# A gated mix of linear attention and a state-space convolution: one group's accumulating transfers, cast and triangle product at other places of the order

## The chip, the cores and the metric

One NeuronCore of one Trainium2 chip runs the kernel. The metric is device time in microseconds (us) of one launch. Three runs of the kernel before gave 176.87, 177.70 and 178.03 us, median 177.7 us.

The core has five engines that each work through their own instructions in order: PE (TensorE, matrix products), ACT (ScalarE), DVE (VectorE), POOL (GpSimd) and SP (SyncE, which here only issues transfers). POOL can issue transfers too. A waiting instruction holds back everything behind it on its engine.

## What is computed

```python
g = sigmoid((x * gate_w).sum(-1, keepdims=True))      # x: 1 x 2048 x 448
# a: linear attention, 16 heads of 28
phi = lambda t: where(t > 0, t + 1, exp(t)) + 1e-6
pq, pk = phi(q), phi(k)                               # q, k, v from x @ wqkv
o = (pq @ sum_s(pk * v)) / (pq @ sum_s(pk) + 1e-6)    # not causal
a = o @ wo
# b: convolution of every channel over all 2048 rows, by FFT in the reference
K = 2 * Re(sum_n C * exp(A * dt * l));  b = conv(x, K) + x * D_skip
out = g * a + (1 - g) * b
```

For the parameters of a channel the kernel tests whether all taps of K are the same number to float32. Where they are, the convolution of that channel is this tap times the running sum of x over the rows. This is what the main path computes; a second function, `general_conv`, runs only if the test fails for some channel.

## The kernel before, in words

The 2048 rows are cut into 16 chunks of 128. Four chunks make a group; chunk 4g+r holds, on partition p, row 512g+4p+r. So the four chunks of a group lie side by side as rows r = 0 to 3 of one partition. float32 products are made from a rounded high part (cast on ACT) and the remainder (subtraction on POOL or DVE), so each projection of a chunk is 11 matrix products of 128x448.

**The main loop** (line 517, c = 2 to 13) does, for each c, on PE: the projection k of chunk c+1 (`project`, L349; its result lies in the PSUM bank "k", for c = 2 and 4 in "v1"), the projection q of chunk c, and the products `do_g(c)` (L425), which add x(c) times the feature phi(k(c)) to four sums. PE is given these three blocks of 11 products one after the other, in every round. Around them stand:

- `load_x(c+3)` (L210): SP loads a later chunk, 512 KB, into one of four buffers.
- `split_t(c+2)` (L250, then L246) and `split_n` (L256, then L246): ACT casts the transposed and the plain chunk, POOL subtracts. `skip(c)` (L262) on POOL puts x times D_skip into y.
- `k_feature`, `k_high`, `k_low` (L376 to L388): two activations on ACT, one DVE pass in place in the bank "k", then the cast `pkh` on ACT and two more DVE passes that read the bank. Until the last of them the bank can't take the next projection k.
- `q_post` (L396 to L403): the same for q, with three or four activations on ACT.
- `steps`: pieces of the test of the taps (`s4d_prepare`). Its last reads of the parameters are the DVE instructions L305, two in c = 2 and two in c = 3.

**The running sum** goes group by group, with five steps whose places in the loop are the subject here:

1. `group_load(g)` (L432, SP): 896 KB of x into a home of the group: `wvo` for group 0, `pq` for 1, `room` for 2, `spare` for 3. Home 1 is the place of the parameters that L305 reads, so its load waits for L305, and SP with it.
2. `running_a(g)` (L436) and `running_b(g)` (L440): accumulating transfers of 448 KB issued by POOL. The first adds rows 0 and 2 to rows 1 and 3, the second adds row 1 to rows 2 and 3. The second waits for the first to land, on POOL.
3. `group_split(g)` (L444 on ACT, L246 on POOL): the high and low part of row 3, the tile `sums`.
4. `group_heads(g)` (L451, PE): a triangle matrix times `sums`, two products; they give what all earlier partitions add.
5. `convolve(c)` (L456, L457, DVE), twice for a group: adds the heads, multiplies by the tap; then `group_add(g)` (L463) adds the group to y by a transfer.

After the loop the kernel closes the sums, forms the attention matrices, and goes through the 16 chunks once more with transposes (L647), products `a` (L673) and the writing of the output.

The order of all instructions is written by hand (`manual_schedule`): each engine gets them in the order of the Python text. Before, group 0 stands in it thus: `running_a(0)` last in c = 2 (after `split_n(4)`), `running_b(0)` in c = 4 after `split_t(6)`, `group_split(0)` in c = 5 between the two activations of k(6) and `pkh(6)`, `group_heads(0)` last in c = 5, `convolve(0)` at the head of c = 6.

Of the kernel before, what the change touches and what calls it, by code (L numbers as in the profile page):

```python
# [32 lines left out]
QW = 512  # L33
EDGE = 16
G = 4
PAIRS = (2, 4, 5, 6)
HALVES = (4, 6, 7, 9)
SMALL = 2.0 ** -70
FLAT = 2.0 ** 35
BIG = 3.4028234e38  # L40
# [107 lines left out]
def gated_mix_kernel(ctx: ExitStack, tc: tile.TileContext, xin, wq_d, wvo_d, abc_d, ldt_d, dsk_d,  # L148
# [58 lines left out]
    def load_x(c):  # L207
        r = xp.tile([P, XC], F32, name="xr", tag="xr")
        turned[c], plain[c] = r[:, :NAT], r[:, NAT:]
        SP.dma_start(out=r, in_=xin[c])  # L210
# [34 lines left out]
    def low(eng, o, r, h):  # L245
        eng.tensor_tensor(out=o, in0=r, in1=h.bitcast(F32), op=ALU.subtract)  # L246

    def split_t(c):
        w = xt[c] = xt_p.tile([P, 2 * NAT], F32R, name="xt", tag="t")
        ACT.copy(w[:, :NAT], turned[c])  # L250
        low(POOL, w[:, NAT:], turned[c], w[:, :NAT])

    def split_n(c, both=True):
        r, w = plain[c], xn_p.tile([P, NX], F32R, name="xn", tag="n")
        xn[c] = w
        ACT.copy(w[:, :XC - NAT], r)  # L256
        if c > 2 and both:
            skip(c)
        low(POOL, w[:, XC - NAT:], r[:, :D], w[:, :D])

    def skip(c):
        POOL.tensor_tensor(out=y[:, c], in0=plain[c][:, :D], in1=dsk, op=ALU.mult)  # L262
# [68 lines left out]
    def pieces(c, wh, wl, n, tag, last=None):  # L331
        o = ps.tile([P, 512], F32, name=tag, tag=tag)
        h, l = ([xt[c][:, i + k * P:i + (k + 1) * P] for k in range(J)] for i in (0, NAT))
        hh, lh, hl = ([(a[k], w[:, k]) for k in range(J)] for a, w in ((h, wh), (l, wh), (h, wl)))
        hl = hl[1:]
        if last == "x":
            seq = hh + hl + lh
        else:
            seq = [p for k in range(J) for p in (hh[k], lh[k])] + hl
            if last and len(last) > 1:  # L340
                seq = [{"h": hh, "l": lh, "w": [None] + hl}[i[0]][int(i[1])] for i in last.split()]
            elif last == "w":
                seq = seq[2:6] + seq[8:9] + seq[6:8] + seq[9:] + seq[:2]

        def run(count):
            for _ in range(min(count, len(seq))):
                a, b = seq.pop(0)
                run.n += 1
                PE.matmul(o[:, :n], lhsT=a, rhs=b, start=run.n == 1, stop=not seq)  # L349
        run.n = 0  # L350
        return o, run

    def project(*args, **kw):
        o, run = pieces(*args, **kw)
        run(11)
        return o
# [16 lines left out]
    def k_feature(c, o):  # L373
        e = tp.tile([P, D], F32, name="e", tag="e")
        pks[c] = o[:, :D]
        ACT.activation(e, pks[c], AF.Relu, scale=-1.0)  # L376
        ACT.activation(e, e, AF.Exp, scale=-1.0)  # L377
        DVE.scalar_tensor_tensor(out=pks[c], in0=pks[c], scalar=1.0, in1=e, op0=ALU.add, op1=ALU.max)  # L378

    def k_high(c):  # L380
        pkh[c] = tp.tile([P, 512], F32R, name="pkh", tag="pkh")[:, EDGE:EDGE + D]
        ACT.add(pkh[c], pks[c], 1e-6)

    def k_low(c):
        pk = pks.pop(c)
        pkl[c] = tp.tile([P, 512], F32R, name="pkl", tag="pkl")[:, EDGE:EDGE + D]
        for o, a, op in ((pkl[c], pkh[c].bitcast(F32), ALU.subtract), (zb, zb, ALU.add))[::-1 if c > 6 else 1]:
            DVE.scalar_tensor_tensor(out=o, in0=pk, scalar=1e-6, in1=a, op0=ALU.add, op1=op)  # L388
# [6 lines left out]
    def q_post(c, o, mid=None):  # L395
        ACT.activation(e1[:, c:c + 1], o[:, D:D + 1], AF.Exp, scale=-1.0)  # L396
        if c < 5 or c >= NC - 2:
            return feature(pq[:, c], o, mid, side[0][:, :D] if 1 < c < 5 else None)
        e = tp.tile([P, D], F32, name="e", tag="e")
        ACT.activation(e, o[:, :D], AF.Relu, scale=-1.0)  # L400
        ACT.activation(e, e, AF.Exp, scale=-1.0)
        ACT.add(e, e, 1e-6)
        DVE.scalar_tensor_tensor(out=pq[:, c], in0=o[:, :D], scalar=C1, in1=e, op0=ALU.add, op1=ALU.max)  # L403
# [27 lines left out]
    def group_load(g):  # L431
        SP.dma_start(out=homes[g], in_=xin[g * G:(g + 1) * G, :, NAT:LO].rearrange("r p d -> p r d"))  # L432

    def running_a(g):
        w = homes[g]
        POOL.dma_start(out=w[:, 1::2], in_=w[:, 0::2], accum_op=ALU.add)  # L436

    def running_b(g):
        w = homes[g]
        POOL.dma_start(out=w[:, 2:], in_=w[:, 1:2].to_broadcast([P, 2, D]), accum_op=ALU.add)  # L440

    def group_split(g):
        w = sums[g] = tp.tile([P, 2, D], F32R, name="sums", tag="v0", bufs=1)
        ACT.copy(w[:, 0], homes[g][:, G - 1])  # L444
        low(POOL, w[:, 1], homes[g][:, G - 1], w[:, 0])

    def group_heads(g):
        o = heads[g] = ps.tile([P, 512], F32, name="v", tag="v0")[:, :D]
        w = sums.pop(g)
        for i in range(2):  # L450
            PE.matmul(o, lhsT=tri, rhs=w[:, i], start=i == 0, stop=i == 1)  # L451

    def convolve(c):
        g, i = c // G, c % G
        a, full = homes[g][:, i:i + 2], [P, 2, D]
        DVE.tensor_tensor(out=a, in0=a, in1=heads[g][:, None, :].to_broadcast(full), op=ALU.add)  # L456
        DVE.tensor_tensor(out=a, in0=a, in1=near[0][:, None, :].to_broadcast(full), op=ALU.mult)  # L457
        if i and g < NC // G - 1:
            for k in (g, UL + g):
                SP.dma_start(out=u[k:k + 1], in_=homes[g][P - 1:P, G - 1])  # L460

    def group_add(g):
        POOL.dma_start(out=y[:, g * G:(g + 1) * G], in_=homes[g], accum_op=ALU.add)  # L463

    prep = s4d_prepare()
    def steps(n):
        for _ in range(n):
            next(prep, None)
# [48 lines left out]
    for c in range(2, NC - 2):  # L517
        if c + 3 < NC:
            load_x(c + 3)
        if c == 2:  # L520
            SP.dma_start(out=cst, in_=cst_d)
        if c == 10:
            SP.dma_start(out=wo, in_=wvo_d[:DJ, 1])
        if c == 11:
            SP.dma_start(out=wv, in_=wvo_d[:, 0])
        ko = project(c + 1, wkh, wkl, D, "v1" if c in (2, 4) else "k")
        if c > 5:
            convolve(2 * c - 12)
        split_t(c + 2)
        if c in HALVES:  # L530
            running_b(HALVES.index(c))
        if c > 5:
            split_n(c + 2, False)
        k_feature(c + 1, ko)
        if c in (5, 7, 9, 11):
            group_split(c // 2 - 2)
        if c > 5:
            skip(c + 2)
        k_high(c + 1)
        k_low(c + 1)  # L540
        qo = project(c, wqh, wql, D + 2, "q")
        q_post(c, qo)
        if c < 5:
            steps(2 if c == 4 else 1)
        if c == 4:
            ACT.copy(tri, trir)
            ACT.copy(gcr, gcat)
        if c == 7:
            SP.dma_start(out=okr[:, None, :DJ], in_=oks[:, None, :])
        if c == 9:  # L550
            DVE.tensor_reduce(out=okr[:, DJ:], in_=okr[:, :DJ], op=ALU.add, axis=AX.X)
            DVE.tensor_copy(okn, okr[:, DJ:])
        do_g(c, (0, 1))
        if c == 5:
            steps(1)
        do_g(c, (2, 3))
        if c in (5, 7, 9, 11):
            group_heads(c // 2 - 2)
        if c < 4:
            skip(c - 1)  # L560
        if c < 6:
            split_n(c + 2)
        if c in (3, 4, 5):
            group_load(c - 2)
        if c in PAIRS:
            running_a(PAIRS.index(c))
        if c in (7, 9, 11, 13):
            group_add(c // 2 - 3)
        for j in {12: (0, 1), 13: (2, 3)}.get(c, ()):
            w = xn_p.tile([P, NX], F32R, name="wo", tag="n") if j < 2 else xp.tile([P, XC], F32R, name="wo", tag="xr")  # L570
            w = w[:DJ, :2 * D].rearrange("p (i d) -> p i d", i=2)
            woh.append(w[:, 0])
            wol.append(w[:, 1])
            ACT.copy(woh[j], wo[:, j])
            low(POOL, wol[j], wo[:, j], woh[j])
# [110 lines left out]
    c = NC - 2  # L686
# [291 lines left out]
```

## Time and profile before

| | |
|---|---|
| median of three runs | 177.7 us (176.87 to 178.03) |
| the profiled execution, its own time | 178.07 us |
| its span, first to last instruction | 176.2 us |
| PE busy | 165.9 us, 94% of the span, 852 matrix products |
| PE weight loads, beside the products | 148.5 us, 84% |
| POOL busy | 119.4 us, 68% |
| DVE busy | 117.2 us, 67% |
| ACT busy | 107.6 us, 61% |
| moved by DMA | 29.45 MB, 7.34 MB of it in transfers issued by POOL |

The profile counts from the span's start. "L246" is a line of the kernel; "xt<-xr" are tiles, written and read. A bracket behind a row gives the idle time of the engine before it and what ended it. The 1.87 us between the execution's own time and its span lie outside the instructions.

### The profile page before, as it was taken

The numbers are of one execution on the slowest core, as the hardware profiler recorded it, in microseconds if no ns is written. First come the engines' busy times: TensorE is split into PE (matmuls) and PEld (weight loads), VectorE is DVE, ScalarE is ACT, GpSimd is POOL, SyncE is SP. The second block draws the span as 40 slices with busy tenths as digits, with TensorE's granted clock in tenths as the row PEclk, the third lists the DMA queues.
The fourth block names the chain that finished last, engine by engine and source line by source line (L and its number), as shares of the span: only waits on it lengthen the run. The fifth ranks groups of instructions, "written<-read, shape, count | busy, mean of one in ns | idle before, by whom it ended". The sixth has DMA issues, their size and how long they took to land.

```text
span 176.2 us, 2710 instructions
## 1 busy us (share of the span) xinstructions
PE 165.9 (94%) x852; PEld 148.5 (84%) x852; DVE 117.2 (67%) x230; ACT 107.6 (61%) x245; POOL 119.4 (68%) x128
## 2 busy tenths in 40 slices
PE   6999999999927999999999999999999999999990
PEld 2698999989915999999999999999879999999990
DVE  0837736598416476585775676877888998997541
ACT  3778488894217669469478586665664564675441
POOL 6082688799517999949837929839886997954000
PEclk9999999999996999999999999999999999999999
DMA  5999997056999999958999820630031221221221
GB/s 178 404 301 272 255 287 293 14 92 179 271 264 346 337 184 195 290 119 173 288 274 302 180 56 0 130 80 0 5 67 54 105 105 57 103 102 57 106 107 57
DMA packets 12186, 29.45 MB, mean 167 GB/s; under 512 B 1549, under 2 KB 8410, under 8 KB 12170
## 3 DMA queue, kind: packets, MB, share of 16 engines
q1 hardware_dynamic: 9274, 21.81, 38.2%
q0 software_dynamic: 2752, 7.34, 21.9%
q8 instruction: 7, 0.11, 0.3%
q10 hardware_dynamic: 144, 0.11, 0.2%
q14 instruction: 9, 0.07, 0.1%
HBM read 17.93 MB, written 3.67 MB: 123 GB/s over the span
## 4 chain that ended last, share of the span: by engine, by line
PE 59%; ACT 8%; DMA 8%; DVE 4%; POOL 3%; issue 2%; SPq 1%; ACTq 0%; POOLq 0%; DVEq 0%
PE a L673 19%; PE q L349 11%; PE g L425 11%; PE k L349 11%; DMA wvo<-wvo 7%; PE tr L647 3%; DMA wk<-shl 2%; ACT y L303 2%; PE v L349 1%; ACT y L304 1%; PE v L451 1%; POOL xt L246 1%; ACT xn L256 1%; SPq L810 1%; POOL xn L246 1%
## 5 line engine op out<-in xcount | busy, mean ns | idle before, releaser
L673 PE MATMUL a<-wk,th 128*128 128x448 f32 (+1 forms) x170 | 36.7, 361 | 0.2 <-DMA wk<-shl 0.2
L425 PE MATMUL g<-pkh,xn 128*128 128x448 f32 x112 | 35.8, 364 | 0.0
L673 PEld LDWEIGHTS a<-wk,th 128*128 128x128 f32 x170 | 29.5, 189 | 2.3 <-issue 0.7
L246 POOL TENSOR_TENSOR xt<-xr,xt 128x512 fp32r<-128x512 f32 x14 | 21.3, 1521 | 12.6 <-ACT xt L250 12.6
L349 PE MATMUL k<-wk,xt 128*128 128x448 f32 x121 | 28.5, 383 | 0.0
L349 PE MATMUL q<-wqh,xt 128*128 128x450 f32 x120 | 27.6, 367 | 0.0
L246 POOL TENSOR_TENSOR xn<-xr,xn 128x448 fp32r<-128x448 f32 x16 | 22.8, 1424 | 4.8 <-ACT xn L256 4.8
L349 PEld LDWEIGHTS k<-wk,xt 128*128 128x128 f32 x121 | 23.9, 198 | 2.4 <-ACT wk L473 0.5
L349 PEld LDWEIGHTS q<-wqh,xt 128*128 128x128 f32 x120 | 22.5, 189 | 1.8
L425 PE MATMUL g<-pkl,xn 128*128 128x448 f32 x64 | 23.4, 366 | 0.0
L425 PEld LDWEIGHTS g<-pkh,xn 128*128 128x128 f32 x112 | 21.1, 188 | 2.2
L262 POOL TENSOR_TENSOR y<-xr,rows 128x448 f32<-128x448 f32 x16 | 22.1, 1414 | 0.0
L585 POOL TENSOR_TENSOR room<-pq,zb 128x448 f32<-128x448 f32 x16 | 18.7, 1173 | 3.8 <-ACT zb L707 2.7
L610 POOL TENSOR_TENSOR room<-pq,den 128x336 f32<-128x336 f32 x16 | 12.3, 769 | 7.5 <-ACT den L599 4.0
L378 DVE SCALAR_TENSOR_TENSOR k<-k,e 128x448 f32<-128x448 f32 x11 | 7.0, 632 | 15.0 <-ACT e L377 15.0
L678 DVE SCALAR_TENSOR_TENSOR ot<-y,og,a 128x448 f32<-128x448 f32 (+1 forms) x17 | 10.7, 629 | 5.5 <-PE a L673 5.5
L376 ACT ACTIVATE e<-k 128x448 f32<-128x448 f32 x11 | 6.0, 544 | 12.3 <-PE k L349 12.3
L655 DVE TENSOR_TENSOR th<-tr,th 128x512 fp32r<-128x512 f32 x16 | 11.0, 690 | 2.6 <-ACT th L654 2.0
L654 ACT CAST th<-tr 128x512 fp32r<-128x512 f32 x16 | 9.4, 588 | 5.1 <-PE tr L647 4.9
L425 PEld LDWEIGHTS g<-pkl,xn 128*128 128x128 f32 x64 | 11.2, 174 | 1.2 <-DVE pkl L388 0.2
L349 PE MATMUL v<-wk,xt 128*128 128x448 f32 x55 | 12.0, 364 | 0.0
L250 ACT CAST xt<-xr 128x512 fp32r<-128x512 f32 x14 | 8.6, 611 | 5.7 <-DMA xr<-in 5.7
(183 smaller groups left out, 321.1 us busy)
## 6 DMA issues: line engine op xcount, KB each, us to landing
xr<-in SPq DMA_DIRECT2D x15, 512.0 KB, 4.4
out<-ot SPq DMA_DIRECT2D x15, 224.0 KB, 1.9
pq<-in SPq DMA_DIRECT2D x4, 448.0 KB, 13.7
wvo<-in SPq DMA_DIRECT2D x2, 896.0 KB, 12.4
y<-in SPq DMA_DIRECT2D x2, 480.0 KB, 4.0
y<-in SPq DMA_DIRECT2D x2, 450.0 KB, 7.8
wvo<-wvo POOLq DMA_DIRECT2D x2, 448.0 KB, 8.2
pq<-in SPq DMA_DIRECT2D x1, 896.0 KB
```

The source lines that it names most:

```text
L246: eng.tensor_tensor(out=o, in0=r, in1=h.bitcast(F32), op=ALU.subtract)
L250: ACT.copy(w[:, :NAT], turned[c])
L262: POOL.tensor_tensor(out=y[:, c], in0=plain[c][:, :D], in1=dsk, op=ALU.mult)
L349: PE.matmul(o[:, :n], lhsT=a, rhs=b, start=run.n == 1, stop=not seq)
L378: DVE.scalar_tensor_tensor(out=pks[c], in0=pks[c], scalar=1.0, in1=e, op0=ALU.add, op1=ALU.max)
L425: PE.matmul(g[i][:a.shape[1], :D], lhsT=a, rhs=b, start=c == 0 and n == 0, stop=c == NC - 1 and n == len(seq) - 1)
L585: POOL.tensor_tensor(out=pd[c], in0=pq[:, c], in1=zb, op=ALU.mult)
L610: POOL.tensor_tensor(out=n[:, :3, :DJ].rearrange("p j (h d) -> p j h d", h=4), in0=a, in1=r[:, :H - 4].rearrange("p (j h) -> p j h", j=3)[ ...
L654: ACT.copy(h, ov)
L655: DVE.tensor_tensor(out=l, in0=ov, in1=h.bitcast(F32), op=ALU.subtract)
L673: PE.matmul(a[:, lo:hi], lhsT=u_, rhs=w_[:, lo:hi], start=n == 0, stop=n == 10)
L678: DVE.scalar_tensor_tensor(out=ot[:, lo:hi], in0=y[:, c, lo:hi], scalar=og[:, c:c + 1], in1=a[:, lo:hi], op0=ALU.mult, op1=ALU.add)
```

## The change

- `running_a(0)` goes a step forward in c = 2: behind the two `skip` passes, ahead of the subtraction of `split_n(4)`. To allow this, `skip(c+2)` is called by itself ahead of `split_n`, in c = 2 and 3.
- `running_b(0)` goes from c = 4 to the same place in c = 3.
- `group_split(0)` goes behind the q work and `split_n(7)` of c = 5; `group_heads(0)` behind the projection k(7) in c = 6; `convolve(0)` behind `k_low(7)`.
- `group_load(2)` and `group_load(3)` go from the end of c = 4 and 5 to the head of c = 5 and 6, behind `load_x(8)` and `load_x(9)`.
- `running_a(2)`, `running_a(3)`, `running_b(2)` and `running_b(3)` move by one step to about one and a half rounds; `running_b(1)` stands in c = 6 as before.

Nothing is computed otherwise, and the number of instructions on every engine is the same. Two constants go, so the helpers' line numbers are 2 lower after the change.

```diff
-PAIRS = (2, 4, 5, 6)
-HALVES = (4, 6, 7, 9)
...
+        if c in (5, 6):
+            group_load(c - 3)
...
         ko = project(c + 1, wkh, wkl, D, "v1" if c in (2, 4) else "k")
-        if c > 5:
+        if c == 6:
+            group_heads(0)
+        if c > 6:
             convolve(2 * c - 12)
         split_t(c + 2)
-        if c in HALVES:
-            running_b(HALVES.index(c))
+        if c == 6:
+            running_b(1)
+        if c in (6, 8):
+            running_a(c // 2 - 1)
         if c > 5:
             split_n(c + 2, False)
         k_feature(c + 1, ko)
-        if c in (5, 7, 9, 11):
+        if c in (7, 9, 11):
             group_split(c // 2 - 2)
+        if c in (7, 9):
+            running_b(c // 2 - 1)
         if c > 5:
             skip(c + 2)
         k_high(c + 1)
         k_low(c + 1)
+        if c == 6:
+            convolve(0)
...
-        if c in (5, 7, 9, 11):
+        if c in (7, 9, 11):
             group_heads(c // 2 - 2)
         if c < 4:
             skip(c - 1)
+            skip(c + 2)
+            (running_a, running_b)[c - 2](0)
         if c < 6:
-            split_n(c + 2)
-        if c in (3, 4, 5):
-            group_load(c - 2)
-        if c in PAIRS:
-            running_a(PAIRS.index(c))
+            split_n(c + 2, c > 3)
+        if c == 3:
+            group_load(1)
+        if c == 4:
+            running_a(1)
+        if c == 5:
+            group_split(0)
```

How the engines' orders move, at three places. First POOL in c = 2 to 4, before (L262 the `skip` passes, L436 and L440 the two accumulating transfers of group 0, L246 the subtractions):

```order
L262 TENSOR_TENSOR y<-xr,rows 128x448 x2
L246 TENSOR_TENSOR xn<-xr,xn 128x448
L436 DMA wvo<-wvo 128x2x448
L246 TENSOR_TENSOR xt<-xr,xt 128x512
L262 TENSOR_TENSOR y<-xr,rows 128x448 x2
L246 TENSOR_TENSOR xn<-xr,xn 128x448
L246 TENSOR_TENSOR xt<-xr,xt 128x512
L440 DMA wvo<-wvo 128x2x448
```

and after (the same helpers at L260, L434, L438, L244):

```order
L260 TENSOR_TENSOR y<-xr,rows 128x448 x2
L434 DMA wvo<-wvo 128x2x448
L244 TENSOR_TENSOR xn<-xr,xn 128x448
L244 TENSOR_TENSOR xt<-xr,xt 128x512
L260 TENSOR_TENSOR y<-xr,rows 128x448 x2
L438 DMA wvo<-wvo 128x2x448
L244 TENSOR_TENSOR xn<-xr,xn 128x448
L244 TENSOR_TENSOR xt<-xr,xt 128x512
```

The first transfer moves past one subtraction, the second past two; both now stand directly behind the `skip` passes.

Second, ACT in c = 5 and the start of c = 6, before. The rows are the cast of x(7) transposed, the two activations of k(6), the cast of group 0's `sums`, `pkh(6)`, the q work of chunk 5, the casts of x(7) plain and x(8):

```order
L250 CAST xt<-xr 128x512
L376 ACTIVATE e<-k 128x448
L377 ACTIVATE e<-e 128x448
L444 CAST sums<-wvo 128x448
L382 ACTIVATE pkh<-k 128x448
...
L402 ACTIVATE e<-e 128x448
L256 CAST xn<-xr 128x512
L250 CAST xt<-xr 128x512
```

and after:

```order
L248 CAST xt<-xr 128x512
L374 ACTIVATE e<-k 128x448
L375 ACTIVATE e<-e 128x448
L380 ACTIVATE pkh<-k 128x448
...
L400 ACTIVATE e<-e 128x448
L254 CAST xn<-xr 128x512
L442 CAST sums<-wvo 128x448
L248 CAST xt<-xr 128x512
```

The cast of `sums` moves from ahead of `pkh(6)` to behind the plain cast of x(7).

Third, PE from the end of c = 5 to the q projection of c = 6, before:

```order
L425 MATMUL g_147<-pkl,xn 64x448
L425 MATMUL g_147<-pkh,xn 128x448
L451 MATMUL v<-sums,tri 128x448 x2
L349 MATMUL k<-wk_70,xt 128x448 x11
L349 MATMUL q<-wqh,xt 128x450 x8
```

and after:

```order
L423 MATMUL g_147<-pkl,xn 64x448
L423 MATMUL g_147<-pkh,xn 128x448
L347 MATMUL k<-wk_70,xt 128x448 x11
L449 MATMUL v<-sums,tri 128x448 x2
L347 MATMUL q<-wqh,xt 128x450 x8
```

The two triangle products now stand behind the eleven products of k(7).

## The prediction

> **What bounds the kernel now.** I read the page's slices first, then PE's own rows, the chain of waits that ended last, and then ACT, POOL, DVE and SP backwards from the one place where PE stands still.
>
> ```profile
> PE   6999999999927999999999999999999999999990
> ```
>
> PE is full in all slices but the first, the last, and one near 50 us. So the end is set by the products, and only what PE waits there can be won. PE's rows at that place, with the wait in brackets:
>
> ```profile
> 49.17 0.37 PE L425 MATMUL g<-pkh,xn 128*128 128x448 f32 x1
> 53.30 0.47 PE L451 MATMUL v<-sums,tri 128*128 128x448 f32 x1 [3.77 <-ACT sums L444]
> 54.53 0.74 PE L451 MATMUL v<-sums,tri 128*128 128x448 f32 x1 [0.75 <-POOL sums L246]
> 55.07 3.62 PE L349 MATMUL k<-wk,xt 128*128 128x448 f32 x11
> 58.53 1.81 PE L349 MATMUL q<-wqh,xt 128*128 128x450 f32 x8
> ```
>
> The triangle products of group 0 wait 3.77 us for the cast of `sums` and 0.75 us for its remainder. The projection behind them is slow as well. The chain says what the cast waited for, and gives the usual price of a projection in its last row:
>
> ```profile
> 41.13 11.49 DMA wvo<-wvo
> ...
> 53.33 1.16 POOL sums L246
> ...
> 55.27 3.42 PE k L349 x11
> ...
> 63.18 2.20 PE k L349 x11
> ```
>
> `running_b(0)`, issued at 41.13, needs 11.49 us to land. The eleven products cost 3.42 us instead of 2.20, and the windows (fifth column from the right POOL's busy time, then granted clock, DMA share, GB/s) show why:
>
> ```profile
> 36.00:38.00 2.00, 2.00 (x11) 1.87 (x11) 1.90 (x3) 1.94 (x8) 1.91 (x2) 1.00 0.77 126
> 38.00:40.00 2.00, 2.00 (x12) 1.84 (x11) 1.97 (x5) 1.59 (x4) 1.81 (x2) 1.00 0.00 0
> ...
> 54.00:56.00 2.00, 1.47 (x4) 1.27 (x5) 1.44 (x4) 1.85 (x4) 1.59 (x3) 0.58 1.06 339
> ```
>
> From 54 to 56 us the granted clock is 0.58, right behind the stall. And from 38 to 40 us, before the transfer is issued, DMA does nothing at all.
>
> **What else is late there.** With the transfer out of the way, something must be next. ACT's rows:
>
> ```profile
> 47.15 0.62 ACT L250 CAST xt<-xr 128x512 fp32r<-128x512 f32 x1 [4.58 <-DMA xr<-in]
> 47.68 0.54 ACT L376 ACTIVATE e<-k 128x448 f32<-128x448 f32 x1
> 48.24 0.58 ACT L377 ACTIVATE e<-e 128x448 f32<-128x448 f32 x1
> 52.68 0.56 ACT L444 CAST sums<-wvo 128x448 fp32r<-128x448 f32 x1 [3.86 <-DMA wvo<-wvo]
> 53.16 0.54 ACT L382 ACTIVATE pkh<-k 128x448 fp32r<-128x448 f32 x1
> ...
> 55.31 0.60 ACT L256 CAST xn<-xr 128x512 fp32r<-128x512 f32 x1
> ```
>
> ACT had already waited 4.58 us for chunk 7 to land, until 47.15. That wait costs PE nothing before, but the change puts the cast of `sums` behind all the work that follows this landing. So the landing of x(7), call it L, is what I have to place. SP's rows:
>
> ```profile
> 40.12 0.38 SPq L432 DMA_DIRECT2D pq<-in  x1
> 40.55 0.50 SPq L210 DMA_DIRECT2D xr<-in  x1
> 41.09 0.43 SPq L432 DMA_DIRECT2D room<-in  x1
> ```
>
> x(7) is issued at 40.55, behind group 1's load at 40.12, and lands 7.03 us after that. Group 1's load waits for the last L305 on DVE. One row groups the four L305, and three rows give the passes behind:
>
> ```profile
> L305 DVE SCALAR_TENSOR_TENSOR y<-pq x4: 683/1106/1523, 30.7 to 38.5; 112x512 f32<-112x512 f32 x4
> ```
>
> ```profile
> 48.86 0.63 DVE L378 SCALAR_TENSOR_TENSOR k<-k,e 128x448 f32<-128x448 f32 x1 [2.54 <-ACT e L377]
> 53.73 0.62 DVE L388 SCALAR_TENSOR_TENSOR pkl<-k,pkh 128x448 fp32r<-128x448 f32 x1 [4.24 <-ACT pkh L382]
> 54.27 0.61 DVE L388 SCALAR_TENSOR_TENSOR zb<-k,zb 128x448 f32<-128x448 f32 x1
> ```
>
> The last L305 starts at 38.5 and ends 1.52 later, at 40.0. The first pair took about 0.69 each, the second 1.52. POOL tells the two apart:
>
> ```profile
> 27.92 2.27 POOL L262 TENSOR_TENSOR y<-xr,rows 128x448 f32<-128x448 f32 x2
> 31.84 1.25 POOL L246 TENSOR_TENSOR xn<-xr,xn 128x448 fp32r<-128x448 f32 x1 [1.64 <-ACT xn L256]
> 33.03 1.33 POOL L436 DMA_DIRECT2D wvo<-wvo  x1
> 33.95 1.75 POOL L246 TENSOR_TENSOR xt<-xr,xt 128x512 fp32r<-128x512 f32 x1
> 35.21 2.69 POOL L262 TENSOR_TENSOR y<-xr,rows 128x448 f32<-128x448 f32 x2
> 38.19 1.28 POOL L246 TENSOR_TENSOR xn<-xr,xn 128x448 fp32r<-128x448 f32 x1 [0.29 <-ACT xn L256]
> ```
>
> At the first pair (30.7 to 32.1) POOL stands idle; at the second (36.9 to 40.0) it runs `skip` and subtractions.
>
> **The change part by part.**
>
> *First transfer forward.* POOL's `skip` pair ends at 27.92 + 2.27 = 30.19 and POOL then idles 1.64 us. The transfer, which holds POOL 0.92 us (33.03 to 33.95), fits in that gap: cost nothing, and xt(5) starts at 33.1 instead of 33.95. Group 0's own load must have landed: the transfers on its home took at most 12.4 us, so it was there by 16.3 + 12.4 = 28.7.
>
> ```profile
> DMA to landing us min/median/max: 4.9/10.3/12.4
> L432 SPq DMA_DIRECT2D wvo<-in x1: 402/402/402, 16.3 to 16.3; - x1
> ```
>
> The best case there, 4.9, is the first transfer: 33.03 + 4.9 = 37.9, where the windows' DMA share drops to 0. Moved to 30.2 it lands at 35.1.
>
> *Second transfer forward.* POOL does xt(5) until 34.3 and the `skip` pair (2.27 when undisturbed) until 36.6, and issues the transfer there; the first has landed 1.5 us before, so POOL waits for nothing. Behind it stand xn(5) (waits for ACT's cast anyway, until 38.1) and xt(6), which ends about 40.6, before k(6) needs it at 42.35. With DMA idle I take 4.9 us, so it lands at 41.5; beside loads it would be 11.49, so 48.1. Both are ahead of the cast's new place (about 51), so the range of this term moves the sum by nothing.
>
> *A side effect, the largest open term.* At 36.9 POOL is now only issuing and then waiting for ACT, so I expect the L305 pair at its short price: 36.94 + 2 x 0.69 + 0.08 = 38.4 instead of 40.0. Group 1's load and x(7) follow 1.55 us earlier. The second transfer is still moving when they start; I give it 0.3 us of theirs (estimate from 41.5 against a start of data near 40.4). L = 47.15 - 1.55 + 0.3 = 45.9. If issuing a transfer disturbs DVE as much as a subtraction does, L stays 47.15. If x(7) isn't disturbed at all, 45.3.
>
> *Cast and triangle product behind.* From L the order of ACT, DVE and POOL gives: 1.71 to the DVE pass of k(6) (47.15 to 48.86), 0.63 + 0.04 to `pkh`, 2.15 through the q work to the plain cast of x(7) (53.16 to 55.31), 0.65 to POOL, 1.15 for xn(7) and 1.16 for the remainder of `sums`, 0.05 to PE: 7.54. The second triangle product starts at 45.9 + 7.5 = 53.4 and q(6) 0.2 later, at 53.6. ACT's cast itself is done at about 51.5.
>
> PE meanwhile ends the products of c = 5 at 49.4. k(7) writes the bank "k" that the DVE passes of k(6) read until `pkh` + 1.72, at 45.9 + 2.38 + 1.72 = 50.0: 0.6 us of stall. k(7) takes 2.20, one triangle product 0.2, at 52.4, then 1.0 us of stall. So the 3.77 + 0.75 us of waiting shrink to about 1.6, and two short gaps stand where one long one was. With them the low clock should go: k(7) at 2.20 instead of 3.42.
>
> **Sum:** q(6) at 53.6 instead of 58.53, 4.9 us earlier. Behind it PE has no wait until the loop's end in the trace, so I carry the 4.9 to the end: span 176.2 - 4.9 = 171.3, the profiled execution 178.07 - 4.9 = 173.2, and the median, which lies 0.4 below that execution, **172.8 us**.
>
> *The clock.* The Trainium skill, "TensorE: Matmul & The Clock Gate", Part 1, says that the array falls to half rate after an idle window of about 3.4 us. The trace agrees: 3.77 us of idleness, then 0.58. By that rule gaps of 0.6 and 1.0 us leave the clock alone; without it the sum would lose up to 3.42 - 2.20 = 1.2.
>
> *Later groups.* The load of `room` goes behind x(8), so x(8) and x(9) come sooner. POOL's two issues in c = 6, 2 x 0.92, lie ahead of xn(8) and xt(9), needed one and two rounds later (6.6 us each). `convolve(0)` ends before the DVE pass of q(6). I cost these at nothing, except for what the second rival says.
>
> **The rivals.**
>
> 1. *x(7) comes no earlier* (L = 47.15): q(6) at 54.9, 3.6 us won, 174.1. For it: the second L305 pair runs beside POOL in the trace. The first transfer landing late belongs here too: at 11.49 us (41.7) POOL would hold back xt(6) and k(6) for 2.8 us, the second transfer lands at 53.2 and q(6) starts at 55.2, 174.4. Against that: DMA share 0 around it.
> 2. *The stall moves to group 1.* `running_b(1)` is reached at about 54.7 on POOL; ACT's cast for it is due at 61.4, and PE's triangle products at 53.6 + 2.2 x 5 = 64.6. The remainder needs 1.8 us after the landing, so landing by 62.8 costs nothing. At 11.49 us it lands at 66.2: 3.3 us lost, 1.6 won, 176.1. It turns **slower** if `running_a(1)` also needs 11.49 us. It is issued once group 1's load has landed, ahead of x(7), so at about 45, behind four loads: POOL then waits until 56.5, the second lands at 68.0, PE stands 5.2 us and the clock falls again for 1.2. That is 1.5 more than the 4.9 won: 179.2. For it: 11.49 is what such a transfer took beside the loads. Against: by 55 the loads of c = 4 to 6 should be through.
> 3. *L far earlier* (44 or less): PE alone sets the pace, 49.4 + 2.20 + 0.4 = 52.0, 6.5 won, 171.2.
>
> The Trainium skill, "DMA: Bandwidth & Descriptors", section "SWDGE vs HWDGE vs iDMA", says that each DMA engine takes turns between the queues of the two kinds of issuer. By it a transfer of 4.9 us beside loads would be some 8 us (estimate: its moving part doubled), and rival 2 would vanish. The 11.49 us of this trace is longer than that, so I keep the rival.
>
> **How the numbers follow.** Forecast (172 to 173.5) 0.66; rival 1 and its like, 0.20; rival 2 at 176.1, 0.06, and slower, 0.04; rival 3, 0.04. A measurement of this kernel tells about 1%, 1.8 us, from no change. Forecast, rivals 1 and 3 are faster by more: 0.90; 176.1 is within: 0.06; slower 0.04. The range takes in rivals 1 and 3 and leaves rival 2 out: 171.2 to 175.2.
>
> **What would show it.** Right: group 1's load issued at 38.5, ACT's cast of xt(7) near 46, k(7) ahead of the triangle products with waits of about 0.6 and 1.0 us, clock 1.00 throughout, q(6) near 53.6 and no new wait before the loop's end. Wrong: L305 still at 1.52, POOL idle ahead of `running_b(0)` or `running_b(1)`, a wait of PE at the triangle products of group 1, or a clock below 1 between 50 and 70 us.

## The result, and the profile after

| | before | after |
|---|---|---|
| median | 177.81 us (176.87 to 178.03) | 173.03 us (172.58 to 173.44), 4 runs |
| ratio | | 0.974, 95% interval 0.9696 to 0.9784 |
| the profiled execution, its own time | 178.07 us | 172.81 us |
| its span | 176.2 us | 170.9 us |
| start of q(6) on PE | 58.53 us | 53.30 us |

The forecast was 172.8 us. The change made the kernel 2.6% faster. First the slices of the page after, PE's row and the granted clock in tenths:

```profile
PE   6999999999988999999999999999999999999990
...
PEclk9999999999999999999999999999999999999999
```

The two slices that had 2 and 7 before have 8 and 8 now. What PE still waits for in the whole span, by engine and line, total, times and longest:

```profile
PE q L266 <- POOL warm L197: 1.3, 1, 1.3
PE k L347 <- DVE zb L386: 0.7, 1, 0.7
PE v L449 <- POOL sums L244: 0.6, 1, 0.6
```

The first line is the start-up. The other two are the two short gaps that the prediction put there. PE's rows at that place:

```profile
49.71 2.44 PE L347 MATMUL k<-wk,xt 128*128 128x448 f32 x11 [0.66 <-DVE zb L386]
52.00 0.36 PE L449 MATMUL v<-sums,tri 128*128 128x448 f32 x1
52.99 0.47 PE L449 MATMUL v<-sums,tri 128*128 128x448 f32 x1 [0.64 <-POOL sums L244]
53.30 1.79 PE L347 MATMUL q<-wqh,xt 128*128 128x450 f32 x8
```

k(7) runs from 49.71 to the next start at 52.00, so 2.29 us, where it had 3.46 (55.07 to 58.53). POOL's rows, the two transfers at their new places, and much later the second transfer of group 1:

```profile
29.91 1.33 POOL L434 DMA_DIRECT2D wvo<-wvo  x1
31.65 1.22 POOL L244 TENSOR_TENSOR xn<-xr,xn 128x448 fp32r<-128x448 f32 x1 [0.41 <-ACT xn L254]
32.84 1.29 POOL L244 TENSOR_TENSOR xt<-xr,xt 128x512 fp32r<-128x512 f32 x1
34.10 2.26 POOL L260 TENSOR_TENSOR y<-xr,rows 128x448 f32<-128x448 f32 x2
36.30 1.18 POOL L438 DMA_DIRECT2D wvo<-wvo  x1
38.02 1.16 POOL L244 TENSOR_TENSOR xn<-xr,xn 128x448 fp32r<-128x448 f32 x1 [0.53 <-ACT xn L254]
...
55.22 1.19 POOL L438 DMA_DIRECT2D pq<-pq  x1 [1.02 <-DMA pq<-pq]
```

The first transfer uses the idle time ahead of xn(4), of which 0.41 us is left. The second is issued without a wait. DVE's two later passes over the parameters, SP's issues behind them and ACT's cast of x(7):

```profile
36.74 0.68 DVE L303 SCALAR_TENSOR_TENSOR y<-pq 112x512 f32<-112x512 f32 x1
...
37.47 0.69 DVE L303 SCALAR_TENSOR_TENSOR y<-pq 112x512 f32<-112x512 f32 x1
```

```profile
38.25 0.38 SPq L430 DMA_DIRECT2D pq<-in  x1
38.68 1.84 SPq L208 DMA_DIRECT2D xr<-in  x2
```

```profile
45.46 0.62 ACT L248 CAST xt<-xr 128x512 fp32r<-128x512 f32 x1 [3.37 <-DMA xr<-in]
...
47.83 0.55 ACT L380 ACTIVATE pkh<-k 128x448 fp32r<-128x448 f32 x1 [0.70 <-DVE k L376]
...
50.51 0.56 ACT L442 CAST sums<-wvo 128x448 fp32r<-128x448 f32 x1
```

The pair that had 1.52 us each has 0.68 and 0.69 now; group 1's load goes out at 38.25 instead of 40.12, and x(7) lands 1.69 us earlier (45.46 instead of 47.15). The cast of `sums` waits for nothing.

**Where the time came from.** q(6) starts 5.23 us earlier, and from q(6) to the end of the span it is 117.7 us before (176.2 - 58.53) and 117.6 after (170.9 - 53.30). So all of it was won ahead of q(6) and none given back behind. The 5.23 us are the 3.77 + 0.75 us of waiting and the slow projection's 1.17, less the two new gaps of 0.66 + 0.64, which makes 4.39. Another 0.48 is an earlier arrival at this place: the last product of c = 5 starts at 48.69 instead of 49.17. The remaining 0.36 lie in the triangle products, whose second row was 0.74 long and is 0.47, and in the pauses beside them.

Not all of the 0.48 is the change's. A POOL row that stands ahead of every moved instruction, before and after:

```profile
25.55 1.16 POOL L246 TENSOR_TENSOR xn<-xr,xn 128x448 fp32r<-128x448 f32 x1 [0.76 <-ACT xn L256]
```

```profile
25.34 1.15 POOL L244 TENSOR_TENSOR xn<-xr,xn 128x448 fp32r<-128x448 f32 x1 [0.76 <-ACT xn L254]
```

So 0.21 us were there before the change could act, and it brought about 5.0 of the 5.23. Over all profiled kernels this row starts between 25.02 and 25.86; so a few tenths between two spans can't be put down to a change. Most of the other 0.27 lies in the projection k(5), from its start to q(4) 2.41 us before (35.45 to 37.86) and 2.19 after (35.19 to 37.38). This fits the remainder xt(5), which ended at 35.70 before (33.95 + 1.75) and at 34.13 now.

### The profile page after: what moved, and what is told of

Its sections match the earlier page's. It is cut to its first block, busy times and chain, and to the rows that moved or that the text cites. A ratio compares the mean times of both kernels' runs of the same rounds, so it can differ in the third digit from the quotient of the medians.

```text
span 170.9 us, 2712 instructions
## 1 busy us (share of the span) xinstructions
PE 163.9 (96%) x852; PEld 146.8 (86%) x852; DVE 115.6 (68%) x230; ACT 107.8 (63%) x245; POOL 118.8 (70%) x128
## 4 chain that ended last, share of the span: by engine, by line
PE 67%; ACT 8%; DMA 4%; POOL 3%; issue 3%; DVE 1%; ACTq 0%; POOLq 0%
PE a L685 21%; PE q L347 13%; PE g L423 13%; PE k L347 9%; PE tr L659 4%; DMA xr<-in 4%; ACT y L301 2%; PE m L762 2%; PE v L347 1%; ACT y L302 1%; PE v L449 1%; ACT xt L248 1%; PE k L782 1%; PE tr L782 1%; ACT xn L254 1%
## 5 line engine op out<-in xcount | busy, mean ns | idle before, releaser
L347 PE MATMUL k<-wk,xt 128*128 128x448 f32 x121 | 27.0, 367 | 0.7 <-DVE zb L386 0.7
L244 POOL TENSOR_TENSOR xn<-xr,xn 128x448 fp32r<-128x448 f32 x16 | 23.1, 1443 | 5.8 <-ACT xn L254 5.7
L244 POOL TENSOR_TENSOR xt<-xr,xt 128x512 fp32r<-128x512 f32 x14 | 21.2, 1514 | 7.3 <-ACT xt L248 7.3
L347 PEld LDWEIGHTS k<-wk,xt 128*128 128x128 f32 x121 | 22.5, 188 | 3.5 <-ACT e L399 1.0
L260 POOL TENSOR_TENSOR y<-xr,rows 128x448 f32<-128x448 f32 x16 | 23.5, 1474 | 0.0
L696 ACT COPY pq<-a 128x448 f32<-128x448 f32 (+1 forms) x17 | 8.7, 517 | 5.0 <-DVE ot L690 5.0
```

What stands on the lines that cost most here:

```text
L696: ACT.copy(pq[:, c, lo:hi], a[:, lo:hi])
```

## The experiments

Each ratio is against the kernel before, run on the same chip. Line numbers are two lower where the constants of the change are gone.

**1. The low clock by itself.** The kernel before, with 19 products of the triangle's size put into the stall, ahead of the real ones that overwrite them.

```diff
+        for _ in range(19 if g == 0 else 0):
+            PE.matmul(o, lhsT=tri, rhs=wkh[:, 1], start=True, stop=True)
         for i in range(2):
             PE.matmul(o, lhsT=tri, rhs=w[:, i], start=i == 0, stop=i == 1)
```

> The kernel before with 19 further triangle-sized products (on finished weights, overwritten by the two real ones) ahead of group 0's triangle products, so that PE is busy during the 3.77 us it waits for the cast; nothing else moves. Theory A, the low clock follows from the long idleness and costs 1.2 us: k(7) takes 2.2 instead of 3.4 us, granted clock 1.00 at 54 to 58 us, 176.5 us against 177.7 of before. Rival B, the clock falls for another reason or costs nothing: 177.7.

176.92 us against 178.42, ratio 0.9934 (0.9895 to 0.9972). PE's rows of this kernel, and the windows with the granted clock behind POOL's column:

```profile
49.16 3.97 PE L451 MATMUL v<-wk,tri 128*128 128x448 f32 x19
...
54.09 0.48 PE L453 MATMUL v<-sums,tri 128*128 128x448 f32 x1 [0.75 <-POOL sums L246]
54.49 2.47 PE L349 MATMUL k<-wk,xt 128*128 128x448 f32 x11
56.80 1.80 PE L349 MATMUL q<-wqh,xt 128*128 128x450 f32 x8
```

```profile
54.00:56.00 2.00, 1.92 (x8) 1.61 (x9) 1.45 (x3) 1.44 (x3) 1.59 (x3) 1.00 1.05 342
```

The cast and the remainder are no earlier than before, yet with PE kept busy the clock stays at 1.00 and k(7) takes 2.31 us (54.49 to 56.80). The span is 175.0, 1.2 us shorter. In all six executions the mean granted clock is 0.994 to 1.00. So about 1.2 us of the 5.3 was the clock's, and PE's idleness in the stall causes it, since nothing else was changed.

**2. The early transfers alone.** The kernel before with `skip` and the two transfers of group 0 moved; cast, triangle products and later groups as before.

```diff
-        if c in HALVES:
+        if c in HALVES[1:]:
             running_b(HALVES.index(c))
...
         if c < 4:
             skip(c - 1)
+            skip(c + 2)
+            (running_a, running_b)[c - 2](0)
         if c < 6:
-            split_n(c + 2)
+            split_n(c + 2, c > 3)
...
-        if c in PAIRS:
+        if c in PAIRS[1:]:
             running_a(PAIRS.index(c))
```

> The kernel before with only the two accumulating transfers of group 0 moved early (and skip(4), skip(5) called ahead of them); cast, triangle products, loads and later groups as before. Theory A: group 0 costs PE nothing, as with the cast put back (q(6) near 51.7, 171.5 us), but POOL has running_a(2), running_a(3) and running_b(2) ahead of group 1's remainder, which with the later groups put back was ready 0.3 us late for PE; PE now comes 1.7 us sooner, so it waits 0.6 to 1.9 us at the triangle products of group 1: 172.1 to 173.4 us, 172.6 taken. Rival B, the later groups' places never matter: 171.5. Rival C, the early transfers alone win little: 176 or more.

172.56 us against 177.94, ratio 0.9702 (0.9675 to 0.9728). The transfers alone bring all that the whole change brings. q(6) starts at 51.80, 1.5 us earlier than in the whole change, but not all of it reaches the end. PE's row at the triangle products of group 1:

```profile
64.16 0.47 PE L451 MATMUL v<-sums,tri 128*128 128x448 f32 x1 [0.90 <-POOL sums L246]
```

Here PE waits for group 1, which it doesn't in the kernel after. ACT's cast of this group had waited 2.17 us, until 61.93, for `running_b(1)` to land, issued at 54.67. That is the second rival's place, with a price of 0.9 us.

**3. The cast back.** The kernel after, with the cast, the triangle products and `convolve(0)` where they were before.

```diff
-        if c == 6:
-            group_heads(0)
-        if c > 6:
+        if c > 5:
             convolve(2 * c - 12)
...
-        if c in (7, 9, 11):
+        if c in (5, 7, 9, 11):
             group_split(c // 2 - 2)
...
-        if c == 6:
-            convolve(0)
...
-        if c in (7, 9, 11):
+        if c in (5, 7, 9, 11):
             group_heads(c // 2 - 2)
...
-        if c == 5:
-            group_split(0)
```

> The changed kernel with the cast of group 0's sums, its triangle products and convolve(0) put back to their places of before (cast between the activations of k(6) and pkh(6), products last in c = 5); the transfers stay early. Theory A, the gain is the earlier landing of the second transfer and the place of the cast wins nothing by itself: the cast fits into ACT's idle 0.7 us ahead of pkh(6) (47.1 to 47.8), its remainder is ready at 48.8, the two triangle products run from 48.9 inside the 0.66 us that PE waits for bank k anyway, and q(6) starts at 51.9 instead of 53.3: 171.7 us against 173.0 of the change. Rival B, the gain is that cast and product lie behind other work: PE waits at the triangle product in c = 5 again and most of the gain is lost, 175 us or more.

171.52 us against 178.38, ratio 0.9615 (0.9571 to 0.9659): faster than the whole change, and the intervals do not touch. PE's rows and ACT's:

```profile
48.56 0.56 PE L449 MATMUL v<-sums,tri 128*128 128x448 f32 x2
49.30 2.47 PE L347 MATMUL k<-wk,xt 128*128 128x448 f32 x11 [0.17 <-DVE zb L386]
```

```profile
46.72 0.55 ACT L442 CAST sums<-wvo 128x448 fp32r<-128x448 f32 x1
47.52 0.55 ACT L380 ACTIVATE pkh<-k 128x448 fp32r<-128x448 f32 x1 [0.24 <-DVE k L376]
```

ACT idles 0.70 us ahead of `pkh(6)` in the kernel after, because DVE's pass has to end first. The cast of 0.55 us fits in there and delays nothing. And PE, which has to wait for the bank "k" anyway, does the triangle products in that time. So with the transfers early, moving the cast behind costs: PE waits 0.17 us here instead of 0.66 + 0.64, and the span is 169.4 instead of 170.9, with 0.32 of this difference there before any moved row (25.02 against 25.34).

**4. x(7) ahead of group 1's load.** The kernel after, with that load behind `load_x(7)`.

```diff
-        if c in (5, 6):
+        if c in (4, 5, 6):
             group_load(c - 3)
...
-        if c == 3:
-            group_load(1)
```

> The changed kernel with group 1's load issued behind load_x(7) instead of ahead of it, so that x(7) no longer waits for the last L305. Theory A, the 0.66 and 0.64 us that PE still waits are set by the landing of x(7): ACT's cast of it falls from 45.5 to about 42, both waits go, q(6) starts at 51.5, 171.3 us (up to 171.8 if the triangle products of group 1 then wait a little for POOL). Rival B, the waits come from ACT's and POOL's own work: 173.0. Rival C, the earlier load delays the first accumulating transfer, which lands at 41 instead of 35; POOL and k(6) are held back by about 2.8 us: 174 or more.

171.38 us against 178.38, ratio 0.9609 (0.9568 to 0.965). No wait of PE is left but the start-up's. ACT's cast of xt(7) and PE's rows:

```profile
41.76 0.63 ACT L248 CAST xt<-xr 128x512 fp32r<-128x512 f32 x1
```

```profile
48.68 2.36 PE L347 MATMUL k<-wk,xt 128*128 128x448 f32 x11
...
51.70 1.78 PE L347 MATMUL q<-wqh,xt 128*128 128x450 f32 x8
```

So both gaps of the kernel after hang on the landing of x(7), as the prediction's chain from L says.

**5. Both of the last two.** The cast back as in 3, and x(7) first as in 4 (the two diffs together).

> The changed kernel with the cast, triangle products and convolve(0) back and x(7) loaded ahead of group 1's load. Theory A: either of the two alone leaves PE with 0.2 us of waiting or none, so both together give what each gives, 171.4 us. Rival B, the two gains (1.5 and 1.6 us) add up: 169.9.

170.86 us against 177.94, ratio 0.9612 (0.9581 to 0.9643). The ratio is that of 3 and of 4: the two edits remove the same two waits of PE, 0.66 + 0.64 us, once. q(6) starts at 51.37, where PE alone would bring it (48.76 for the triangle products, 49.16 for k(7), no wait between). By its profiled span, 169.0, this is the shortest of all kernels run, though 4 and 3, at 169.3 and 169.4, can't be told from it.

**6. The cast alone.** The kernel before with only the cast, the triangle products and `convolve(0)` moved as in the change.

```diff
+        if c == 6:
+            group_heads(0)
-        if c > 5:
+        if c > 6:
             convolve(2 * c - 12)
...
-        if c in (5, 7, 9, 11):
+        if c in (7, 9, 11):
             group_split(c // 2 - 2)
...
+        if c == 6:
+            convolve(0)
...
-        if c in (5, 7, 9, 11):
+        if c in (7, 9, 11):
             group_heads(c // 2 - 2)
...
+        if c == 5:
+            group_split(0)
```

> The kernel before with only the cast, the triangle products and convolve(0) of group 0 moved behind (the cast's step ahead of running_a(2) on POOL); transfers and loads as before. Theory A: x(7) still lands at 47.15 and running_b(0) at 52.6, the cast starts there, the remainder is ready at 54.7, q(6) starts at 54.9: 3.6 us below before, 174.2 us. Rival B, the transfers' places are the whole gain: PE still stalls about 3 us and the clock falls, 176.5 or more. Rival C, the order of cast and products is the whole gain: 173.0.

177.01 us against 178.38, ratio 0.9936 (0.9896 to 0.9976). The expectation was missed: a good part of the gain is lost again one round later. ACT's and PE's rows there, in the profiled execution:

```profile
57.23 0.62 ACT L250 CAST xt<-xr 128x512 fp32r<-128x512 f32 x1 [3.58 <-DMA xr<-in]
```

```profile
62.00 4.01 PE L349 MATMUL k<-wk,xt 128*128 128x448 f32 x11 [2.17 <-DVE pkl L388]
```

x(8), issued behind the load of `room`, lands only at 57.2. In the kernel before it is about as late (its cast starts at 56.82), under cover of the stall. The work of k(7) on ACT stands behind its cast, and k(8) waits 2.17 us for it. In this execution k(8) then runs at the low clock, but this is the slowest of the ten, 178.55 us. Three of them (178.24 to 178.55) have a mean granted clock of 0.984 to 0.988; the other seven (176.27 to 177.13) have 0.994 to 1.00. So the median of 177.01 does not hold the price of the low clock. That the wait of 2.17 us stands in the other seven too is likely, but no profile shows it. The next kernel tests whether x(8) is the cause.

**7. Cast and later groups, without the early transfers.** The kernel after, with the two transfers of group 0 where they were. Beside 6 it has the later groups' loads and transfers moved, x(8) ahead of `room` among them.

```diff
-        if c == 6:
-            running_b(1)
+        if c in (4, 6):
+            running_b(HALVES.index(c))
...
-            skip(c + 2)
-            (running_a, running_b)[c - 2](0)
         if c < 6:
-            split_n(c + 2, c > 3)
+            split_n(c + 2)
...
-        if c == 4:
-            running_a(1)
...
+        if c in (2, 4):
+            running_a(PAIRS.index(c))
```

> The changed kernel with both accumulating transfers of group 0 put back (running_a(0) last in c = 2, running_b(0) in c = 4); cast, triangle products and the later groups' loads stay as changed, so against the kernel with only the cast moved, x(8) now lands ahead of room's load. Theory A, that kernel lost to the late x(8) alone: here the second wait at k(8) and its low clock are gone, L305 takes 1.52 us twice, x(7) is cast near 47.2, q(6) starts at about 54.9, 174.4 us. Rival B, the transfers' places cost more than that (PE waits again before q(6), or at k(8)): 176 us or more. Against the kernel with only running_a(0) back, which has the same order otherwise, it also shows whether running_b(0) ahead of xn(5) made the last L305 take 4.95 us: 1.52 here says yes.

174.27 us against 178.42, ratio 0.9756 (0.9718 to 0.9794). x(8) is there in time (its cast starts at 53.41 without a wait), and the loss of 6 is gone. DVE's group, ACT's cast of xt(7) and PE's two waits:

```profile
L305 DVE SCALAR_TENSOR_TENSOR y<-pq x4: 684/1107/1524, 30.9 to 38.7; 112x512 f32<-112x512 f32 x4
```

```profile
47.03 0.62 ACT L250 CAST xt<-xr 128x512 fp32r<-128x512 f32 x1 [4.26 <-DMA xr<-in]
```

```profile
51.28 2.45 PE L349 MATMUL k<-wk,xt 128*128 128x448 f32 x11 [1.54 <-DVE zb L388]
...
54.78 0.47 PE L451 MATMUL v<-sums,tri 128*128 128x448 f32 x1 [0.75 <-POOL sums L246]
55.09 1.18 PE L349 MATMUL q<-wqh,xt 128*128 128x450 f32 x5
```

This is the prediction's first rival: the second pair at 1.52 us, x(7) at 47.03, q(6) at 55.09, where the rival had 47.15, 54.9 and 174.1 us.

**8. The later groups back.** The kernel after, with the loads and transfers of groups 2 and 3 at their old places.

```diff
-        if c in (5, 6):
-            group_load(c - 3)
...
-        if c == 6:
-            running_b(1)
-        if c in (6, 8):
-            running_a(c // 2 - 1)
+        if c in (6, 7, 9):
+            running_b((6, 7, 9).index(c) + 1)
...
-        if c in (7, 9):
-            running_b(c // 2 - 1)
...
-        if c == 3:
-            group_load(1)
-        if c == 4:
-            running_a(1)
+        if c in (3, 4, 5):
+            group_load(c - 2)
         if c == 5:
             group_split(0)
+        if c in (4, 5, 6):
+            running_a(c - 3)
```

> The changed kernel with the later groups put back (loads of room and spare ahead of x(8) and x(9), the accumulating transfers of groups 2 and 3 at their places of before, running_a(2) behind the remainder of sums). Theory A, by the run with only the cast moved: x(8) lands later here too, ACT's cast of it, due at 51, waits up to about 52.5 since no accumulating transfer shares the queues until then, which PE's 2 us of slack at k(8) still covers; 173.0 to 173.6 us. Rival B, the later groups' places matter as much as there: x(8) lands near 56, PE waits about 2 us at k(8) and the clock falls, 176 us.

173.32 us against 178.42, ratio 0.9722 (0.9689 to 0.9755), against 0.974 for the whole change: no difference that can be told. Beside the early transfers these moves bring nothing; they are needed in 6 (without them, 2.7 us are lost), and in 2, where PE arrives at group 1 earlier. The expected wait for x(8) did not come: it stands behind the load of `room` here as in 6, and is cast at 50.90 without a wait. So this order of the loads does not make x(8) late by itself; it did so with group 0's transfers late. Why, was not tried.

**9. The first transfer back.** The kernel after, with `running_a(0)` behind xn(4) again and `running_b(0)` left early.

```diff
-            (running_a, running_b)[c - 2](0)
+            if c == 3:
+                running_b(0)
         if c < 6:
             split_n(c + 2, c > 3)
+        if c == 2:
+            running_a(0)
```

> The changed kernel with running_a(0) alone put back behind the subtraction of split_n(4). Theory A, moving it freed POOL from work during the second L305 pair: now POOL's skip pair runs beside L305 again, the pair takes 1.52 us each, group 1's load is issued near 39.9 instead of 38.25, x(7) is cast near 47.1, and q(6) starts at 54.9: 174.6 us. Rival B, L305 was slow for another reason, or x(7) does not set the pace: 173.0. In both the second transfer still lands in time.

176.91 us against 178.38, ratio 0.9931 (0.9899 to 0.9963): worse than expected by over 2 us. DVE's last pass and POOL's rows:

```profile
38.04 4.95 DVE L303 SCALAR_TENSOR_TENSOR y<-pq 112x512 f32<-112x512 f32 x1
```

```profile
37.70 1.21 POOL L438 DMA_DIRECT2D wvo<-wvo  x1 [0.26 <-ACT xn L254]
38.48 1.61 POOL L244 TENSOR_TENSOR xn<-xr,xn 128x448 fp32r<-128x448 f32 x1
39.60 1.73 POOL L244 TENSOR_TENSOR xt<-xr,xt 128x512 fp32r<-128x512 f32 x1
40.86 1.57 POOL L260 TENSOR_TENSOR y<-xr,rows 128x448 f32<-128x448 f32 x1
```

A pass of 0.69 us takes 4.95 while POOL goes from one subtraction to the next, and ends at 42.99, 0.56 us after POOL has run out of work (40.86 + 1.57 = 42.43). The `skip` pair ends 1.1 us later here than in the kernel after, so the transfer's issue fills the time in which POOL otherwise waits for xn(5). In experiment 7 POOL's order is the same up to there, without the second transfer ahead of xn(5), and this pass takes 1.52 us. x(7) then lands at 49.23, 3.8 us later than in the kernel after.

**10. POOL's gap filled.** To test that reading: the kernel after with both transfers early, and one more POOL product of 128x448 behind the second, whose output is never used.

```diff
             (running_a, running_b)[c - 2](0)
+            if c == 3:
+                POOL.tensor_tensor(out=spare[:, 0], in0=plain[c][:, :D], in1=dsk, op=ALU.mult)
```

> The changed kernel with one further pass on POOL (a 128x448 product into the unused home of group 3) right behind running_b(0), so that POOL works without a gap while the second L305 pair is due. Theory A, a DVE pass that reads two SBUF operands is kept out for as long as POOL works without a gap: the last L305 takes about 4.9 us, as in the run with running_a(0) back, k(6) and x(7) come 3 to 4 us later, 176.9 us. Rival B, it only takes 1.52 us beside POOL: group 1's load is issued at 39.1, x(7) is cast near 46.3, 173.9. Rival C, the pass is in nobody's way: 173.0.

176.87 us against 178.42, ratio 0.9917 (0.9885 to 0.9949). The time is as expected; the pass that is held is the first of the pair and not the last. DVE's row, POOL's first and last rows of the stretch, and PE's projection q(5):

```profile
36.58 5.97 DVE L303 SCALAR_TENSOR_TENSOR y<-pq 112x512 f32<-112x512 f32 x1
```

```profile
36.93 1.61 POOL L572 TENSOR_TENSOR spare<-xr,rows 128x448 f32<-128x448 f32 x1
...
40.41 1.58 POOL L260 TENSOR_TENSOR y<-xr,rows 128x448 f32<-128x448 f32 x1
```

```profile
47.01 3.34 PE L347 MATMUL q<-wqh,xt 128*128 128x450 f32 x8 [2.93 <-DVE sums L288]
```

One POOL operation of 1.6 us, for which POOL seemed to have time, takes 4.1 of the 5.3 us away (spans of 175.0 and 170.9).

## Why the prediction was right

By its own steps:

- **First transfer at no cost, landing early:** right. It was issued at 29.91 (30.2 in the prediction), xt(5) started at 32.84 (33.1), and the second transfer, at 36.30 (36.6), waited for nothing.
- **Second transfer at 4.9 us, landing at 41.5:** right. The profile's list of DMA issues, with the count, the size of each and the median to landing, has

```profile
wvo<-wvo POOLq DMA_DIRECT2D x2, 448.0 KB, 5.1
```

so, with 5.1 for the median of the two, it landed at about 41.4. In experiment 3 the cast stands at 46.72 and does not wait either.
- **The side effect on the DVE passes**, called the largest open term: right. They take 0.68 and 0.69 us, though the transfer's issue runs beside the first. Experiment 7 is the other bound, 1.52 us each and 174.27. What this term is worth is the step between the two. q(6) starts at 55.09 there and at 53.30 here, 1.79 us apart, of which 0.41 stood before any moved row (25.75 against 25.34). The whole times show less: experiments 7 and 8, on one chip, ran 174.27 and 173.32, and the ratios of experiment 7 and of the whole change, 0.9756 and 0.974, can't be told apart.
- **L at 45.9:** measured 45.46, though x(7) was slowed. From the issue of group 1's load to ACT's cast it is 7.21 us (38.25 to 45.46), before 7.03 (40.12 to 47.15): 0.18 us more, where 0.3 were allowed. L is early because that load went out at 38.25 and not at 38.57 (40.12 - 1.55), and 0.20 of this is only the earlier start of the L305 pair, 36.74 instead of 36.94, which came from the kernel's start. The prediction's bound of 45.3 for an undisturbed x(7) does not follow from its own terms, which give 47.15 - 1.55 = 45.6.
- **The waits of 0.6 and 1.0 us:** measured 0.66 and 0.64. From L to the second triangle product, 7.54 us were forecast and 7.53 measured (45.46 to 52.99). That second wait came out shorter because its end follows L, which came earlier, while PE came to it at 52.36, as forecast (52.4).
- **The clock:** right. It stays at 1.00 and k(7) takes 2.29 us; experiment 1 prices it at 1.2 us by spans.
- **q(6) at 53.6 and the sum of 4.9:** measured 53.30 and 5.23, the span 5.3. The difference is L. By own times it is 5.26, by medians 4.78. That the median of 173.03 lies so close to 172.8 is partly luck: the profiled execution came out at 172.81, below the forecast 173.2, and the median lies 0.22 above it, where the prediction took it 0.4 below.
- **Later groups at nothing, nothing given back behind q(6):** right for this kernel (experiment 8).
- **The second rival:** its first sign is in the profile after, POOL's 1.02 us ahead of `running_b(1)`. The transfer ahead of it, `running_a(1)`, issued at 44.68, holds it until 55.22. It cost PE nothing, since ACT comes to group 1's cast only at 61.20 there, and does not wait. In experiment 2, which reaches group 1 sooner and loads `room` ahead of x(8), it costs 0.9 us.

Where it fell short, though the time was right: the sum never asked what each part was worth beside the others. The early transfers do the work. With them, the cast's move costs PE 1.1 us of waiting (1.30 against 0.17 in experiment 3) instead of helping; the rows for this stood in the trace of before, where `pkh(6)` waits for the DVE pass that ends at 49.49 while the cast would have been through. And the bad end of the side effect was too mild. It was 1.52 us a pass, taken from the nearest rows; experiments 9 and 10 show 4.95 and 5.97 for the same pass. The range would not have held these. That POOL only issues and then waits at that point was right in the text, but 1.1 us more on POOL (experiment 9) end that.

## What to carry to other kernels

Price the parts of a change against each other, not only against the kernel before: two cures for one stall don't add up, and the second can cost what the first no longer needs. Before a cast is moved behind other work, look for idle time of its engine at the old place and for a wait of the consumer that comes anyway. Where DVE reads two operands from SBUF beside a busy POOL, look for the place at which POOL's next row starts only after the last has ended: one more instruction on an engine that is off the path can hold such a pass over several of POOL's rows, as in experiments 9 and 10.

## What the runs showed of the hardware

**A DVE pass beside POOL.** The same pass (112x512, two operands in SBUF) took 0.68 to 0.69 us with POOL idle or only issuing a transfer, 1.52 twice in the kernel before, and 4.95 and 5.97 in experiments 9 and 10. The two of the kernel before:

```profile
36.94 1.52 DVE L305 SCALAR_TENSOR_TENSOR y<-pq 112x512 f32<-112x512 f32 x1
...
38.51 1.52 DVE L305 SCALAR_TENSOR_TENSOR y<-pq 112x512 f32<-112x512 f32 x1
```

With the POOL rows quoted here and in the prediction, all the held passes end at one distance from the end of a POOL row:

| pass | starts | POOL row before its end | that row ends | pass ends | distance |
|---|---|---|---|---|---|
| before, third | 36.94 | `skip` pair, 35.21 + 2.69 | 37.90 | 38.46 | 0.56 |
| before, fourth | 38.51 | xn(5), 38.19 + 1.28 | 39.47 | 40.03 | 0.56 |
| experiment 9, fourth | 38.04 | `skip`, 40.86 + 1.57 | 42.43 | 42.99 | 0.56 |
| experiment 10, third | 36.58 | `skip`, 40.41 + 1.58 | 41.99 | 42.55 | 0.56 |

This reads as if DVE did nothing of the pass until POOL lets it in, and then all of it (0.56 us is a little less than the 0.68 of a free pass, and the ends of POOL's rows are rough). In the last two cases the ends of several POOL rows go by without letting it in. In experiment 9 each next row of POOL starts some 0.5 us ahead of the end of the one before (38.48 + 1.61 = 40.09, and the next starts at 39.60); at the place where the fourth pass before got in, the rows meet (39.47 and 39.44). That this overlap is what shuts DVE out fits these rows, but was not tried by itself.

The Trainium skill, "SBUF — State Buffer", section "Who interferes with whom", says that a DVE instruction with two inputs in SBUF contends with a GpSimd instruction that reads SBUF. The four rows agree. Of a DVE instruction in a two-port mode the section says that whoever issues first gets the shared ports for the whole instruction and that the other is fully blocked. No row tells whether this pass runs in such a mode. The rows look like blocking too, but not by one instruction: the longest single POOL row in these stretches is 1.73 us, and the held rows are 4.95 and 5.97 long. And DVE's row starts first, at 36.58 against 36.93 for POOL's product in experiment 10 and at 38.04 against 38.48 for xn(5) in experiment 9, and is held all the same, as far as the starts of POOL's rows can be trusted.

**The clock.** Where it falls was not sharp in these runs. In the profiled executions it fell behind the stall of 3.77 us before, and behind waits of 2.17 us (experiment 6) and 2.93 us (experiment 10), but not behind one of 2.46 us (experiment 9). The same kernel can go both ways: the mean granted clock of an execution is 0.984 to 0.988 in three of the ten of experiment 6 and 0.994 to 1.00 in the others, and in experiment 9 it is 0.985 to 0.987 in four of ten and 0.993 to 1.00 in the others. The windows of the three profiled ones, with the clock in the third column from the right, in this order:

```profile
62.00:64.00 2.00, 2.00 (x5) 1.79 (x6) 1.97 (x3) 1.42 (x3) 2.00 (x3) 0.50 1.14 211
```

```profile
48.00:50.00 2.00, 2.00 (x7) 1.78 (x6) 1.34 (x9) 0.51 (x1) 1.20 (x1) 0.50 1.02 418
```

```profile
46.00:48.00 2.00, 1.28 (x6) 1.23 (x7) 1.76 (x9) 0.00 (x0) 0.73 (x1) 1.00 1.06 416
```

In the third of them the clock is 1.00 from 48 to 50 us too. The Trainium skill, "TensorE: Matmul & The Clock Gate", Part 1, gives an idle window of about 3.4 us; by it, none of these three waits would have lowered the clock, and two of them did. For the waits of this kernel after, 0.66 and 0.64 us, it makes no difference.

**Accumulating transfers.** From issue to landing the two of group 0 took 5.1 us at the median in the kernel after, and `running_a(1)`, issued behind the loads of x(7) to x(10) and of groups 2 and 3 (the last at 43.34), some 10.5 us (44.68 until POOL goes on at 55.22). For group 0, part of the time passes before any byte moves: its second transfer is issued at 36.30, the DMA share is 0.00 from 36 to 38 us, and 1.08 to 1.11 from 38 to 41. Whether waiting in a queue or the moving takes the 10.5 us was not tried.
